# Rounding the queries and keys of one head one loop step later, in a fused causal attention and maxout FFN

## The chip, the cores and the metric

The kernel runs on 1 core of a Trainium2 chip. The metric is device time in microseconds (us), lower is better. Of the kernel before, three timed runs and one profiled execution are at hand.

## The reference

```python
# q, k, v: 8 batches x 8 heads x 576 x 64; s: 8 x 8 x 576; float32
scores = scale * np.matmul(q, k.transpose(0, 1, 3, 2))
cum = np.cumsum(np.maximum(s, 0.0), axis=-1)
bias = -(cum[:, :, :, None] - cum[:, :, None, :])
scores = np.where(causal, -1000000000.0, scores + np.minimum(bias, 0.0))
attn = np.exp(scores - np.max(scores, axis=-1, keepdims=True))
attn = attn / (np.sum(attn, axis=-1, keepdims=True) + 1e-09)
x = np.matmul(attn, v)                        # then 4608 tokens x 512
h = np.maximum(np.maximum(x @ w1, x @ w2), x @ w3)   # 512 -> 768
out = h @ w_out                                      # 768 -> 512
```

All 64 heads go through attention with a bias that decays with the distance, and the 4608 tokens then through a maxout layer of three matrices and an output matrix.

## The kernel before, in words

**Visits and steps.** Two heads are worked on together, a pair. A visit is one pair and a list of query blocks (128 queries each, the fifth 64): the first eight visits take blocks 0 and 1 of the first two batches, the next eight take their blocks 2, 3 and 4, and the last 24 visits ("stacked") take all five blocks of one pair. One query block of one visit is a step, 160 steps in all. The steps that matter here are 38 and 39 (blocks 3 and 4 of visit 15, the last that is not stacked), 40 to 44 (visit 16, the first stacked visit) and 45 to 49 (visit 17, the second).

**What a step is.** In turn t of the loop at L929 the kernel writes down, for all engines at once and in a fixed order: `probs(t)` (ACT rounds the normalized probabilities to a high float16 half `prh`, L512, and for block 4 a tail `tl`; DVE makes the low half `prl`, L515; SP's queue starts the DMA transposes of both into `ph` and `pl`, L518 to L528); `highest(t + 1)` (DVE, the row maximum, L457 or L462); the evictions that stand open (ACT L593 and L730, DVE L594 and L733, POOL L722 and L723); at most one group of FFN matmuls; `scores(t + 2)` (TensorE, L380, L391, L416); `expo(t + 1)` (ACT, L472 and L477); then a list of single jobs that a table `todo` holds for turn t; then more FFN groups, and after a visit's last block of a phase `values` (TensorE, L584, attention times values, from the transposed `ph`, `pl` and `tT`). Each engine runs its part strictly in this order, and so does SP's DMA queue. The scores live in PSUM in a ring of two buffers (`ps_s`), so `scores(t + 2)` writes the buffer that `probs(t)` has read last. `prh` and `prl` have two buffers each.

**What is prepared for a stacked visit, and when.** Each of its two heads j is loaded and rounded by itself. `load_head` (L121) starts two DMAs on SP's queue into a `raw` tile, of which there are two in a ring. `head_bias` (L128) fills bias rows of `l` with four POOL instructions (L141 to L147). `head_qhi` (L154, ACT) rounds the queries to `h`, `head_khi` (L158, ACT) the keys. `head_qlo` makes what the rounding of the queries left (L163, DVE) and copies a part of `h` into `l` (L167, POOL). `head_klo` makes the rest of the keys (L172, POOL); it is the last to read `raw`. The loop at L872 puts these jobs into `todo`: with o a turn number worked out from the visit's first step, at o `head_bias` and `head_qhi`, at o + 1 `head_khi` and `head_qlo`, at o + 2 `head_klo`, and the load one to three turns ahead of o. For the second stacked visit (n = 1, visit 17, whose first step is 45) head 0 has o = 37 and its load stands at 36.

**The FFN** runs as groups of 12 or 18 matmuls (L716 for the hidden layer, `pm`; L758 for the output, `po`) that a queue hands out by a count of estimated TensorE time; that count is worked out while the program is written, so it is the same in both kernels.

The loop that places the jobs is this, of the function printed below:

```python
for f, e in ((prep4, 1), (prep5, 0), (load, 7), (prep2, 4), (prep3, 3)):
    for v in range(len(visits)):
```

## Time and profile before

| what | value |
|---|---|
| median of three runs | 919.92 us (918.94 to 921.08) |
| the profiled execution | 914.14 us |
| its span, first to last instruction | 912.3 us |
| granted TensorE clock, mean | 0.963 |
| busy: TensorE, its weight loads, DVE, ACT, POOL | 90%, 71%, 66%, 62%, 38% |
| HBM over the span | 60.18 MB read, 9.44 MB written |

PE is TensorE, PEld its weight loads, DVE is VectorE, ACT ScalarE, POOL GpSimd, and SPq the queue of SyncE, from which nearly all DMAs start. A row of the timeline is: start, length, engine, line, operation, output<-input, shape, count, and in brackets the idle time of that engine just before it with what ended it. The chain of waits is followed back from the last instruction. Time outside the span is 914.14 - 912.3 = 1.84 us.

### The profile page before, as it was taken

The page shows a single profiled execution, that of the slowest core. Times are in us where ns is not written, and L with a number is a line of the kernel's source. Part 1 is how long each engine was busy: PE and PEld are TensorE (multiplying, and loading weights), DVE is VectorE, ACT ScalarE, POOL GpSimd, SP SyncE. Part 2 cuts the span into 40 slices and gives each one's busy share as a digit, 9 for nine tenths or more (in the row PEclk, how much of TensorE's full clock was granted, in tenths as well). Part 3 has the DMA queues.
Part 4 walks back from the last instruction along what each step waited for, and adds up shares of the span by engine and source line. Part 5 has one row for each costly group of instructions (what it writes and reads, how often), then busy time and mean ns, then how long its engine had stood idle before and what let it go on. Part 6 is the DMA issues. An engine that isn't in the chain of part 4 may idle for free.

```text
span 912.3 us, 19899 instructions
## 1 busy us (share of the span) xinstructions
PE 823.0 (90%) x7000; PEld 645.5 (71%) x7000; DVE 598.3 (66%) x1504; ACT 568.6 (62%) x1502; POOL 345.7 (38%) x553
## 2 busy tenths in 40 slices
PE   3557769998799989999999999999999999999998
PEld 2445657775467668867787778777787778777876
DVE  6898886666467766667676767676677657663111
ACT  4668577675566776666767677666677677764111
POOL 3111322223434444545353544445344536431211
PEclk9856989999999998999999999999999999999999
DMA  8963346666769768777878867777877677744000
GB/s 292 282 183 79 73 98 138 148 140 128 155 129 166 143 148 140 145 125 139 161 142 160 141 153 143 142 135 146 131 160 153 131 141 135 126 76 83 8 19 29
DMA packets 242036, 122.33 MB, mean 134 GB/s; under 512 B 217808, under 2 KB 226512, under 8 KB 241936
## 3 DMA queue, kind: packets, MB, share of 16 engines
q1 hardware_dynamic: 237904, 108.74, 60.8%
q10 hardware_dynamic: 4032, 12.32, 4.1%
q8 instruction: 55, 0.90, 0.5%
q14 instruction: 45, 0.37, 0.2%
HBM read 60.18 MB, written 9.44 MB: 76 GB/s over the span
## 4 chain that ended last, share of the span: by engine, by line
PE 69%; DMA 5%; DVE 4%; ACT 3%; issue 2%; POOL 2%; SPq 1%; ACTq 0%; DVEq 0%; POOLq 0%
PE pm L716 38%; PE po L758 13%; PE av L584 7%; PE s L380 6%; DMA ph<-prh 2%; PE s L391 2%; DMA pl<-prl 2%; DVE prl L515 2%; ACT prh L512 2%; PE s L416 1%; DVE m L733 1%; SPq L524 1%; POOL hh L722 1%; ACT s L472 1%; POOL hl L723 1%
## 5 line engine op out<-in xcount | busy, mean ns | idle before, releaser
L716 PE MATMUL pm<-x,w 128*128 128x256 f16 (+1 forms) x3456 | 455.9, 289 | 4.3 <-DVE m L733 2.2
L716 PEld LDWEIGHTS <-w 128*128 128x128 f16 x3456 | 330.9, 99 | 95.1 <-issue 8.9
L722 POOL CAST hh<-m 128x256 f16<-128x256 f32 (+1 forms) x96 | 55.4, 578 | 368.8 <-DVE m L733 310.3
L512 ACT ACTIVATE prh<-s,ri 128x512 f16<-128x512 f32 (+3 forms) x288 | 142.0, 539 | 80.8 <-DVE ri L496 71.6
L515 DVE SCALAR_TENSOR_TENSOR prl<-s,ri,prh 128x512 f16<-128x512 f32 (+3 forms) x288 | 152.9, 568 | 58.2 <-ACT prh L512 36.5
L733 DVE SCALAR_TENSOR_TENSOR m<-pm,m 128x256 f32<-128x256 f32 (+1 forms) x192 | 87.2, 454 | 125.1 <-PE pm L716 105.1
L472 ACT ACTIVATE s<-s,nm 128x512 f32<-128x512 f32 (+4 forms) x288 | 151.2, 525 | 12.3 <-DVE nm L457 5.6
L758 PE MATMUL po<-hh,w 128*128 128x256 f16 (+1 forms) x768 | 150.3, 288 | 0.0
L758 PEld LDWEIGHTS <-w 128*128 128x128 f16 x1152 | 110.4, 98 | 33.2 <-issue 5.0
L457 DVE CUSTOM_DVE_ANT_0 s<-s,later 128x128 f32<-128x128 f32 (+1 forms) x192 | 94.7, 493 | 33.4 <-PE s L380 30.0
L758 PE MATMUL po<-hl,w 128*128 128x320 f16 (+1 forms) x384 | 110.3, 287 | 1.5 <-POOL hl L723 1.4
L730 ACT ACTIVATE m<-pm 128x256 f32<-128x256 f32 (+1 forms) x96 | 39.1, 407 | 92.5 <-PE pm L716 88.2
L723 POOL TENSOR_TENSOR hl<-m,hh 128x256 f16<-128x256 f32 (+1 forms) x96 | 75.8, 790 | 7.8
L172 POOL TENSOR_TENSOR l<-raw,h 64x576 fp32r<-64x576 f32 x48 | 67.2, 1401 | 14.2 <-ACT h L158 12.8
L766 ACT ACTIVATE o<-po,os 128x256 f32<-128x256 f32 (+1 forms) x64 | 31.9, 499 | 62.2 <-PE po L758 53.2
L584 PE MATMUL av<-pl,vh 128*64 128x320 f16 (+3 forms) x384 | 59.6, 281 | 8.1 <-DMA pl<-prl 8.0
L462 DVE TENSOR_REDUCE nm<-s 128x1 f32<-128x576 f32 (+3 forms) x64 | 49.9, 780 | 22.1 <-PE s L396 12.3
L584 PEld LDWEIGHTS <-vh 128*64 128x64 f16 x832 | 47.8, 112 | 22.4 <-issue 11.1
L380 PE MATMUL s<-h 128*128 128x128 f32 (+1 forms) x192 | 54.2, 364 | 8.6 <-DVE prl L515 6.2
L584 PE MATMUL av<-ph,vh 128*64 128x320 f16 (+3 forms) x384 | 59.2, 288 | 1.1 <-DMA ph<-prh 0.8
L141 POOL CAST l<-kb 64x576 fp32r<-64x576 f32 x48 | 32.2, 672 | 73.2 <-PE s L391 71.9
L472 ACT ACTIVATION_READ_ACCUMULATOR s<-s,nm 128x1 f32 x288 | 57.3, 199 | 0.0
(140 smaller groups left out, 1090.3 us busy)
## 6 DMA issues: line engine op xcount, KB each, us to landing
raw<-in_qk_dram SPq DMA_DIRECT2D x96, 304.0 KB, 4.7
r<-in_w_dram ACTq DMA_DIRECT2D x20, 512.0 KB, 4.8
rv<-in_qkv_dram SPq DMA_DIRECT2D x32, 320.0 KB, 3.4
out_dram<-o SPq DMA_DIRECT2D x32, 160.0 KB, 2.1
out_dram<-o SPq DMA_DIRECT2D x32, 128.0 KB, 2.0
raw<-in_qkv_dram SPq DMA_DIRECT2D x8, 480.0 KB, 4.1
ph<-prh SPq DMA_TRANSPOSE x192, 3.4
pl<-prl SPq DMA_TRANSPOSE x192, 2.9
```

Of the source, the lines that this page charges most:

```text
L172: nc.gpsimd.tensor_tensor(out=l[far, QP:V0], in0=raw[far, QP:V0], in1=h[far, QP:V0].bitcast(F32), op=ALU.subtract)
L380: nc.tensor.matmul(ps[:, j, :nk], lhsT=w[:, qs], rhs=w[:, QP:QP + nk], start=(x == "h"), stop=(x == "l"), skip_group_check=True,)
L457: nc.vector.tensor_tensor_reduce(out=sc[:, j], in0=sc[:, j], in1=future[0][:, Q4 - nk:Q4], scale=-1.0, scalar=3.0e38, op0=ALU.add, op1=ALU ...
L472: nc.scalar.activation(out=sc, in_=sc, func=AF.Exp, bias=nm[:, j:j + 1], scale=-1.0 if below(t) else 1.0, accum_out=sm[:, j:j + 1],)
L512: nc.scalar.activation(out=hi, in_=src, func=AF.Copy, scale=sc)
L515: nc.vector.scalar_tensor_tensor(out=lo, in0=src, scalar=sc, in1=hi, op0=ALU.mult, op1=ALU.subtract)
L584: nc.tensor.matmul(av[j * D:(j + 1) * D, c0:nq], lhsT=lt, rhs=rt, start=(n < 2), stop=(n >= len(todo) - 2), skip_group_check=True,)
L716: nc.tensor.matmul(pm[:, :nq], lhsT=w[:, wt, kt, :], rhs=xt, start=(n == 0), stop=(n == 3 * NKT - 1))
L722: nc.gpsimd.tensor_copy(out=st["hh"][:, ft, :nq], in_=m1[:, :nq])
L723: nc.gpsimd.tensor_tensor(out=st["hl"][:, ft, :nq], in0=m1[:, :nq], in1=st["hh"][:, ft, :nq], op=ALU.subtract)
L733: nc.vector.scalar_tensor_tensor(out=m1[:, :nq], in0=pm[:, :nq], scalar=HSC, in1=m1[:, :nq], op0=ALU.mult, op1=ALU.max)
L758: nc.tensor.matmul(pm[:, :nq], lhsT=W[18 + ft][:, wt, dt, :], rhs=st[ht][:, ft, :nq], start=(n == 0), stop=(n == 3 * NFT - 1),)
```

## The change

Two lines are new and one is altered, all in the placing of the jobs:

```diff
                     o = first[v] - (8, 5)[j]
                     if n == 0:
                         o += 2 - j
+                    elif n == 1 and j == 0:
+                        o += 1
                     if f is load:
-                        at(o - (1 if n == 1 and j == 0 else 3 if n == 0 and j == 0 else 2), load_head, v, j)
+                        at(o - (3 if n == 0 and j == 0 else 2), load_head, v, j)
                     elif f is prep2:
                         at(o, head_bias, v, j)
                         at(o, head_qhi, v, j)
                         at(o + 1, head_khi, v, j)
                     else:
                         at(o + 1, head_qlo, v, j)
                         at(o + (1 if n == 0 else 2), head_klo, v, j)
```

For head 0 of visit 17 o becomes 38. The load stays in turn 36 (38 - 2 for 37 - 1). `head_bias` and `head_qhi` go from turn 37 to 38, `head_khi` and `head_qlo` from 38 to 39, `head_klo` from 39 to 40. SP's queue and TensorE keep their order; ACT, DVE and POOL do not. No instruction is added or removed.

On ACT, from the end of turn 37 on, before (`h_0` is the head that is moved, `h_1` head 1 of visit 16; the two `prh` are those of steps 38 and 39):

```order
L158 ACTIVATE h_1_3175<-raw_1_3004 128x576
L154 ACTIVATE h_0_3246<-raw_0_3172 128x640
L512 ACTIVATE prh_3287<-s_3149,ri_3285 128x4x128 x2
L593 ACTIVATE x_1_2829<-av_1_3256 128x320
L472 ACTIVATE s_3223,sm_3317<-s_3223,nm_3224 128x576
L477 ACTIVATE se_3319<-sm_3317 128x1
L730 ACTIVATE m_1_4_3321<-pm_1_4_0_3298 128x320
L158 ACTIVATE h_0_3246<-raw_0_3172 128x576
L512 ACTIVATE prh_3344<-s_3223,ri_3342 128x512
L512 ACTIVATE tl_3346<-s_3223,ri_3342 128x64
```

And now, in the same place:

```order
L158 ACTIVATE h_1_3175<-raw_1_3004 128x576
L512 ACTIVATE prh_3280<-s_3149,ri_3278 128x4x128 x2
L593 ACTIVATE x_1_2829<-av_1_3249 128x320
L472 ACTIVATE s_3223,sm_3310<-s_3223,nm_3224 128x576
L477 ACTIVATE se_3312<-sm_3310 128x1
L730 ACTIVATE m_1_4_3314<-pm_1_4_0_3291 128x320
L154 ACTIVATE h_0_3319<-raw_0_3172 128x640
L512 ACTIVATE prh_3341<-s_3223,ri_3339 128x512
L512 ACTIVATE tl_3343<-s_3223,ri_3339 128x64
```

The rounding of the queries, L154, has gone from ahead of the probabilities of step 38 to ahead of those of step 39, and L158 of the same head has left this stretch (it stands ahead of the probabilities of step 40). L163 on DVE has gone the same way.

On POOL, before, from turn 37 to the bias rows of the next head (`l_0` is the moved head, `l_1_3176` head 1 of visit 16, `l_1_3452` head 1 of visit 17):

```order
L141 CAST l_0_3247<-kb_175 64x576
L142 CAST l_0_3247<-qr_178 64x512
L146 MEMSET l_0_3247 64x64
L147 CAST l_0_3247<-qr_178 64x64
L167 CAST l_1_3176<-h_1_3175 64x640
L172 TENSOR_TENSOR l_1_3176<-raw_1_3004,h_1_3175 64x576
L167 CAST l_0_3247<-h_0_3246 64x640
L722 CAST hh_1_2901<-m_1_4_3321 128x320
L723 TENSOR_TENSOR hl_1_2902<-m_1_4_3321,hh_1_2901 128x320
L172 TENSOR_TENSOR l_0_3247<-raw_0_3172,h_0_3246 64x576
L141 CAST l_1_3452<-kb_175 64x576
```

And now, up to the same head's L172:

```order
L167 CAST l_1_3176<-h_1_3175 64x640
L172 TENSOR_TENSOR l_1_3176<-raw_1_3004,h_1_3175 64x576
L141 CAST l_0_3320<-kb_175 64x576
L142 CAST l_0_3320<-qr_178 64x512
L146 MEMSET l_0_3320 64x64
L147 CAST l_0_3320<-qr_178 64x64
L722 CAST hh_1_2901<-m_1_4_3314 128x320
L723 TENSOR_TENSOR hl_1_2902<-m_1_4_3314,hh_1_2901 128x320
L167 CAST l_0_3320<-h_0_3319 64x640
L141 CAST l_1_3451<-kb_175 64x576
L142 CAST l_1_3451<-qr_178 64x512
```

The four bias instructions of the moved head stand behind L167 and L172 of visit 16 instead of ahead of them, its L167 behind an FFN pair instead of ahead of it, and its L172 (not shown) behind the four bias instructions of the next head instead of ahead of them. On SP's queue the load of visit 18's head 0, in turn 40, waits for that L172, since it takes the same `raw` buffer.

Of the kernel before, what the change touches and what calls it, by code (L numbers as in the profile page):

```python
# [21 lines left out]
def kernel(  # L22
# [95 lines left out]
    def stacked(v):  # L118
        return len(visits[v][2]) == 5
# [99 lines left out]
    for j in range(2):  # L219
        nc.gpsimd.memset(ones[64 * j + 32:64 * j + 64, 0:1], 1.0)  # L220
        nc.gpsimd.memset(ones[64 * j:64 * j + 32, 1:2], 1.0)
        for T in range(2):
            a = 32 * j + 16 * T
            for c in range(2):
                o = 32 + 64 * j + 16 * c
# [594 lines left out]
    def at(t, f, *a):  # L820
        todo.setdefault(t, []).append((f, a))
# [50 lines left out]
    for f, e in ((prep4, 1), (prep5, 0), (load, 7), (prep2, 4), (prep3, 3)):  # L872
        for v in range(len(visits)):
            t = first[v] - e
            if v % NP == 0 and f in (prep4, prep5):
                t = first[v] + 1 + (f is prep5) if v else -1
            if f is prep5 and v >= NP and v + NP < len(visits):
                at(t, f, v)
                at(t, load_v, v + NP)
                continue  # L880
            if f is load and NP <= v < 2 * NP:
                t = first[v] - 6
            if 2 * NP * NB - 2 <= v < 2 * NP * NB and f in (load, prep2, prep3):
                t = first[v] - (8 if f is load else 4 if f is prep3 and v % 2 == 0 else 5)
            if stacked(v) and f in (load, prep2, prep3):
                n = v - 2 * NP * NB
                for j in range(2):
                    o = first[v] - (8, 5)[j]
                    if n == 0:
                        o += 2 - j  # L890
                    if f is load:
                        at(o - (1 if n == 1 and j == 0 else 3 if n == 0 and j == 0 else 2), load_head, v, j)
                    elif f is prep2:
                        at(o, head_bias, v, j)
                        at(o, head_qhi, v, j)
                        at(o + 1, head_khi, v, j)
                    else:
                        at(o + 1, head_qlo, v, j)
                        at(o + (1 if n == 0 else 2), head_klo, v, j)
                continue  # L900
            at(t, f, v, *([nc.scalar.dma_start] if f is load and v < NP + 2 else []))
# [121 lines left out]
```

## The prediction

> **What bounds the kernel now.** I read the page first, then the chain of waits, then the waits, the granted clock and the timeline around the place where the moved instructions stand.
>
> ```profile
> PE 823.0 (90%) x7000; PEld 645.5 (71%) x7000; DVE 598.3 (66%) x1504; ACT 568.6 (62%) x1502; POOL 345.7 (38%) x553
> ...
> PE 69%; DMA 5%; DVE 4%; ACT 3%; issue 2%; POOL 2%; SPq 1%; ACTq 0%; DVEq 0%; POOLq 0%
> ```
>
> TensorE sets the pace over most of the span: it is busy 90% of it and holds 69% of the chain. Time saved elsewhere counts only where TensorE stands idle for it. The moved instructions run between 239 and 260 us. The chain of waits there:
>
> ```profile
> 242.66 4.57 DMA raw<-in_qk_dram
> ...
> 247.98 1.26 ACT prh L512 x2
> ...
> 249.26 1.42 DVE prl L515 x2
> 250.68 0.14 issue
> 250.82 1.09 PE s L380 x4
> 251.91 4.63 PE pm L716 x24
> 256.54 0.47 PE s L380 x4
> 257.01 3.29 PE pm L716 x24
> ...
> 275.95 0.50 PE s L380 x4
> ```
>
> The chain leaves TensorE for a load of `raw`, which lands at 242.66 + 4.57 = 247.23, goes over ACT's `prh` and DVE's `prl` of step 38, and comes back to TensorE at 250.82 with `scores(40)`. The waits between 239 and 251 us say the same:
>
> ```profile
> ACT h L154 <- DMA raw<-in_qk_dram: 7.6, 1, 7.6
> DVE prl L515 <- ACT prh L512: 6.9, 1, 6.9
> ...
> PE s L380 <- DVE prl L515: 5.3, 1, 5.3
> ```
>
> The `raw` that lands is that of visit 17, which TensorE does not need until step 45. ACT takes its instructions in order, so L154, waiting for this load, holds up `prh` of step 38 behind it, whose inputs have long been there. That is the wait which the change takes from this place. The timeline of TensorE, then of ACT:
>
> ```profile
> 242.19 0.30 PE L584 MATMUL av<-pl,vh 128*64 128x320 f16 x1 [1.45 <-DMA pl<-prl]
> ...
> 243.68 1.80 PE L716 MATMUL pm<-x,w 128*128 128x320 f16 x12
> ...
> 262.99 0.33 PE L584 MATMUL av<-ph,vh 128*64 128x320 f16 x2
> 263.15 0.30 PE L584 MATMUL av<-pl,vh 128*64 128x320 f16 x2
> ```
>
> ```profile
> 239.06 0.67 ACT L158 ACTIVATE h<-raw 128x576 fp32r<-128x576 f32 x1
> 247.34 0.74 ACT L154 ACTIVATE h<-raw 128x640 fp32r<-128x640 f32 x1 [7.60 <-DMA raw<-in_qk_dram]
> ...
> 251.90 0.69 ACT L512 ACTIVATE prh<-s,ri 128x512 f16<-128x512 f32 x1 [0.49 <-DVE ri L496]
> ```
>
> TensorE ends its group at 243.68 + 1.80 = 245.48 and starts `scores(40)` at 250.82: 5.34 us idle. Between 239.73 and 247.34 ACT does nothing. The clock that TensorE is granted in the stages around it (third column from the right):
>
> ```profile
> 246.00:250.80 4.80, 0.00 (x0) 0.01 (x1) 1.54 (x3) 3.43 (x9) 0.72 (x1) 0.68 0.77 162
> 250.80:252.00 1.20, 1.18 (x6) 1.08 (x7) 1.12 (x4) 0.71 (x3) 0.00 (x0) 0.50 0.95 174
> 252.00:257.00 5.00, 5.00 (x30) 3.37 (x29) 2.52 (x9) 1.84 (x7) 0.00 (x0) 0.75 1.02 200
> ```
>
> After the idle time TensorE runs at half its clock and on the whole at 0.75 for the next 5 us, so the stall costs more than its own length.
>
> **The change part by part.** All times of the new run are worked out on the profiled execution, by moving these rows.
>
> *The idle time.* With L154 gone from ahead of it, `prh` of step 38 waits for the reciprocal `ri` on DVE, and then `scores(40)` for `prl` of step 38 and for `l` of visit 16's head 1, which POOL's L172 finishes. Rows of DVE, then of POOL:
>
> ```profile
> 241.58 0.17 DVE L496 RECIPROCAL ri<-se 128x2 f32<-128x2 f32 x1
> ...
> 250.98 0.81 DVE L163 SCALAR_TENSOR_TENSOR h<-raw,h 64x640 fp32r<-64x640 f32 x1
> ...
> 252.82 0.75 DVE L515 SCALAR_TENSOR_TENSOR prl<-s,ri,prh 128x512 f16<-128x512 f32 x1
> 253.49 0.27 DVE L515 SCALAR_TENSOR_TENSOR tl<-s,ri,tl 128x64 f16<-128x64 f32 x1
> ...
> 256.57 0.49 DVE L733 SCALAR_TENSOR_TENSOR m<-pm,m 128x320 f32<-128x320 f32 x1 [1.06 <-PE pm L716]
> 256.98 0.81 DVE L293 TENSOR_REDUCE am<-rv 128x1 f32<-128x640 f32 x1
> ...
> 258.63 0.61 DVE L515 SCALAR_TENSOR_TENSOR prl<-s,ri,prh 128x128 f16<-128x128 f32 x2
> ```
>
> ```profile
> 242.15 0.66 POOL L141 CAST l<-kb 64x576 fp32r<-64x576 f32 x1
> ...
> 243.57 0.71 POOL L167 CAST l<-h 64x640 fp32r<-64x640 f32 x1
> 244.25 1.39 POOL L172 TENSOR_TENSOR l<-raw,h 64x576 fp32r<-64x576 f32 x1
> ```
>
> `ri` ends at 241.75; 1.26 us of `prh`, 1.42 of `prl` and 0.14 of issue give 244.57. L172 ends at 245.64 now; the four bias instructions ahead of it (242.15 to 243.57, 1.42 us) go behind it, so it ends at 244.22. Both are ahead of 245.48, so the whole 5.34 us go.
>
> *The clock.* Without the idle time the four score matmuls take the 0.50 us of their like at 275.95 instead of 1.09, and the 24 matmuls 3.29 us (the next 24, at 257.01) instead of 4.63: 0.59 + 1.34 = 1.93 us. The Trainium skill, "TensorE: Matmul & The Clock Gate", Part 1: The HAM clock gate, says that the array's clock is halved after an idle window of about 3.4 us and restored after a busy one of the same length. The 0.50 after 5.34 us agrees; by the page the stall would cost 3.4 x 0.5 = 1.7 us of clock, an estimate, and the total below would be 4.8 in place of 5.0.
>
> So TensorE is ahead by up to 5.34 + 1.93 = 7.27 us. Three things are late next.
>
> *L154 in its new place, ahead of `prh` of step 39.* It still waits for the load, which nothing moves (SP's order is the same and no row ahead of 242 us changes): it starts at 247.34, `prh` of step 39 at 247.98. From the start of `prh` to the end of the tail on DVE it is 253.76 - 251.90 = 1.86 us, with the issue 249.98. TensorE is ready for `scores(41)` at 245.48 + 0.50 + 3.29 = 249.27. New idle time: 0.71 us.
>
> *L163 and L158 one step later.* L163 now stands ahead of the reciprocal of step 40. From the FFN eviction at 256.57 to the end of `prl` of step 40 at 259.24 it is 2.67 us, with L163's 0.81 in it 3.48. The two evictions follow the tail (249.84) at once, the second after 0.41 (256.57 to 256.98): `prl` ends at 249.84 + 0.41 + 3.48 = 253.73, with issue 253.87. TensorE gets to `scores(42)` at 249.98 + 0.47 + 3.29 = 253.74. New idle time: 0.13 us. L158 (0.67 us on ACT) stands ahead of `prh` of step 40, which waits for that reciprocal in any case: nothing.
>
> *SP's queue.* The attention values of visit 15 need the transposes of step 39, and SP can't give back all of the stall:
>
> ```profile
> 237.65 2.48 SPq L524 DMA_TRANSPOSE pl<-prl  x2
> ...
> 246.36 0.57 SPq L111 DMA_DIRECT2D rv<-in_qkv_dram  x1
> 249.25 1.25 SPq L518 DMA_TRANSPOSE ph<-prh  x1
> ...
> 255.90 2.48 SPq L524 DMA_TRANSPOSE pl<-prl  x2
> ...
> 262.33 1.97 SPq L125 DMA_DIRECT2D raw<-in_qk_dram  x2
> ```
>
> SP was issuing other transfers until 246.93 and waited only from there to 249.25, so its row moves up by 2.32 us, and the last `pl` of step 39 is issued by 258.38 - 2.32 = 256.06. In step 36 such a transpose was issued by 240.13 and let TensorE go on at 242.19, 2.06 us later; here that is 258.12. TensorE gets to its first `pl` matmul at 263.15 - (7.27 - 0.71 - 0.13) = 256.72. New idle time: 1.40 us, short of the stall that it replaces.
>
> *The bias rows and L172 of the moved head.* POOL has them done long before visit 17's first step; that SP's load for visit 18 (262.33) now waits for this L172 is weighed below.
>
> The sum: 5.34 + 1.93 - 0.71 - 0.13 - 1.40 = 5.03 us. From there on every engine is ahead by this much and all orders are as before, so it should reach the end. The profiled execution, 914.14, would become 909.1. The median of the runs shown is 5.78 above it; I leave that difference as it is: 919.92 - 5.0 = 914.9.
>
> Bounds of what the trace does not show: the new waits could be nothing, 7.27 us in all; or the sixteen DMA engines, not SP's issue, set when `pl` lands. They were idle for 23% of 4.8 us ahead of 250.8, 1.10 us, and full behind it (0.95, 1.02), so the landing would move up by 1.10 instead of 2.32 and the sum be 3.8. I take SP's figure, since in step 36 the landing followed the issue by 2.06 us, with the issue rows back to back.
>
> **The rivals.** *All of it stays:* 7.27 us, 912.6, if `pl` lands 1.4 us earlier than in step 36 and `raw` 0.7 earlier. Against it: SP's rows have no gap to close after 249.25.
>
> *DMA-bound:* 3.8 us, 916.1, as above. For it speaks the share of 1.02, against it that TensorE at 262.99 did not wait for `ph` or `pl`, so that there was room.
>
> *Taken back later:* the gain is given back at a transfer that TensorE waits for further on (5% of the chain is DMA): 919.9. Against it: those transfers are issued out of the same rows that move up.
>
> *Slower, by the load behind L172.* SP's load for visit 18 can't start before the moved head's L172 on POOL, and the transposes of step 41 stand behind it on SP. POOL does the FFN pair and L167, then four bias instructions (1.42 us) and L172 (1.39): it starts the pair at about 250.7 when DVE has evicted (249.84 + 0.41 + 0.49), and even at 2 us for pair and L167 (an estimate from its 0.71 us for L167) ends by 255.6. SP reaches the load at 262.33 - 2.32 = 260.0. It decides only if POOL is over 4.4 us later than that, and the kernel is slower than before by 1.84 us only at 4.4 + 5.0 + 1.84 = 11.3 us: then 921.8 or more. No row near it speaks for that.
>
> That the change does nothing is excluded: the order on ACT is another one, and the wait stood there.
>
> **How the numbers follow.** The forecast, 914.9, has 0.58; DMA-bound 0.16; all of it stays 0.09; taken back 0.12; slower 0.05. A measurement of this kernel can tell 0.2%, 1.84 us, from no change. The range goes from all of it (912.6) to DMA-bound (916.1); the runs shown lie up to 1.2 us from their median, and half of a later loss (2.5 us of 5.0) ends at 917.4, so I give 912.4 to 917.8; 0.17 is left out. Faster: 0.58 + 0.16 + 0.09 = 0.83, and of the loss taken back in part 0.02 more, 0.85; same 0.10; slower 0.05.
>
> **What would show it.** In the new profile: TensorE's idle time ahead of `scores(40)` gone, with the clock near 1 from 245 to 257 us; ACT's wait for `raw` still there, ahead of `prh` of step 39, about 1.5 us long; a wait of TensorE for `pl` ahead of the values of visit 15 near 257 us. The reading is wrong if `scores(40)` still waits for `prl`, if the load of `raw` lands later than 247.3, or if the lead of TensorE at 270 us is well under 4 and the span shows it again at a wait further on.

## The result, and the profile after

| | kernel before | changed kernel |
|---|---|---|
| median of the runs, first comparison | 919.43 us (917.26 to 921.08, 4 runs) | 912.76 us (912.39 to 914.09, 4 runs) |
| ratio | | 0.9937, 95% interval 0.9909 to 0.9964 |
| second comparison | 917.64 us (15 runs) | 912.65 us (8 runs) |
| ratio | | 0.9954, 0.9934 to 0.9975 |
| the profiled execution | 914.14 us | 913.03 us |

The changed kernel is faster, by 5.8 us by the first ratio and 4.2 by the second, and neither interval reaches 1. The two profiled executions differ by 1.11 us alone, which has to be explained too. The page after:

```profile
PE 824.4 (90%) x7000; PEld 646.9 (71%) x7000; DVE 599.1 (66%) x1504; ACT 570.2 (63%) x1502; POOL 346.3 (38%) x553
...
PE 67%; DMA 6%; DVE 4%; ACT 4%; issue 2%; POOL 2%; SPq 1%; POOLq 0%; DVEq 0%; ACTq 0%
```

As a whole it reads as before. The chain of waits around the place does not:

```profile
242.78 2.25 PE av L584 x23
245.03 2.65 PE pm L716 x12
247.69 0.39 PE s L380 x4
248.08 3.29 PE pm L716 x24
...
256.13 3.97 DMA pl<-prl
260.11 0.04 issue
260.15 1.57 PE av L584 x23
```

The load of `raw` has left the chain: `scores(40)` (247.69) follows its FFN group at once, and the 24 matmuls behind it take 3.29 us where they took 4.63. What holds TensorE next is `pl` of step 39. The timeline of TensorE's score and value matmuls, with its idle times in brackets:

```profile
247.42 0.44 PE L380 MATMUL s<-h 128*128 128x128 f32 x2
...
251.09 0.51 PE L380 MATMUL s<-h 128*128 128x256 f32 x2
...
255.55 0.59 PE L380 MATMUL s<-h 128*128 128x384 f32 x2 [0.44 <-ACT s L472]
...
260.15 0.30 PE L584 MATMUL av<-pl,vh 128*64 128x320 f16 x1 [1.57 <-DMA pl<-prl]
```

5.34 us of idle time are gone, 0.44 and 1.57 are new (`scores(42)` and the values of visit 15). ACT in the same stretch:

```profile
239.45 0.67 ACT L158 ACTIVATE h<-raw 128x576 fp32r<-128x576 f32 x1
242.01 1.27 ACT L512 ACTIVATE prh<-s,ri 128x512 f16<-128x512 f32 x2 [1.90 <-DVE ri L496]
...
248.12 0.73 ACT L154 ACTIVATE h<-raw 128x640 fp32r<-128x640 f32 x1
248.75 0.68 ACT L512 ACTIVATE prh<-s,ri 128x512 f16<-128x512 f32 x1
```

`prh` of step 38 runs at 242.01 instead of 247.98, and L154, in its new place, finds its load landed.

To see how far a gain lasts, each execution is cut at the row `se` on ACT, of which every step has one. These are steps 38, 43 and 64, of before and then of after:

```profile
238.96 0.20 ACT L477 ACTIVATE se<-sm 128x2 f32<-128x2 f32 x1
...
271.63 0.20 ACT L477 ACTIVATE se<-sm 128x2 f32<-128x2 f32 x1
...
370.46 0.20 ACT L477 ACTIVATE se<-sm 128x1 f32<-128x1 f32 x1
```

```profile
239.33 0.21 ACT L477 ACTIVATE se<-sm 128x2 f32<-128x2 f32 x1
...
268.62 0.20 ACT L477 ACTIVATE se<-sm 128x2 f32<-128x2 f32 x1
...
369.71 0.20 ACT L477 ACTIVATE se<-sm 128x1 f32<-128x1 f32 x1
```

The differences of these starts, in us, for every profiled execution of the study (the last column goes to the end of the span):

| execution | start to 38 | 38 to 43 | 38 to 64 | 64 to end |
|---|---|---|---|---|
| before | 238.96 | 32.67 | 131.50 | 541.86 |
| before, again | 239.09 | 34.39 | 134.62 | 541.36 |
| bias rows alone | 243.62 | 32.61 | 134.16 | 541.53 |
| changed | 239.33 | 29.29 | 130.38 | 541.51 |
| changed, again | 236.94 | 29.58 | 130.23 | 541.45 |
| other data | 241.09 | 28.95 | 128.25 | 541.63 |
| L154 alone | 238.24 | 28.69 | 130.16 | 541.41 |
| load earlier | 240.75 | 28.87 | 129.06 | 541.48 |
| both heads later | 239.88 | 27.46 | 129.23 | 542.60 |
| L163 and L167 back | 239.82 | 28.24 | 129.13 | 542.15 |
| both of these | 240.09 | 28.01 | 130.84 | 543.34 |
| load later | 242.50 | 37.40 | 136.00 | 541.86 |
| L172 later | 238.45 | 29.03 | 140.12 | 542.09 |

Up to step 38 the executions scatter over 6.7 us, though all but the one with the earlier load are alike there. After step 64 most lie within half a microsecond. The change shows in the middle columns: 33.2 us from 38 to 43 in the first three rows, which have the stall, 29.4 in the two of the changed kernel, 27.5 to 29.6 in the eight rows from the changed kernel to both of these, which do not. From 38 to 64 the means are 133.4 and 129.7, 3.8 us apart. Between 43 and 64 the four with the stall (the load one turn later among them) take 99.8 us in the mean, 98.6 to 101.6, and the eight without it 101.0, 99.3 to 102.8: a part of the gain seems to go again there, within the scatter. So a single pair of profiled executions can hide the gain: the one of before that was shown is the shortest of its three from 38 to 64, and the changed one lost time again near 284 us, as told below. The two last rows of the table are the ones made slower, and are told with their experiments.

### The profile page after: what moved, and what is told of

It reads as the page before. It is cut to its first block, busy times and chain, and to the rows that moved or that the text cites. A ratio compares the mean times of both kernels' runs of the same rounds, so it can differ in the third digit from the quotient of the medians.

```text
span 911.2 us, 19898 instructions
## 1 busy us (share of the span) xinstructions
PE 824.4 (90%) x7000; PEld 646.9 (71%) x7000; DVE 599.1 (66%) x1504; ACT 570.2 (63%) x1502; POOL 346.3 (38%) x553
## 4 chain that ended last, share of the span: by engine, by line
PE 67%; DMA 6%; DVE 4%; ACT 4%; issue 2%; POOL 2%; SPq 1%; POOLq 0%; DVEq 0%; ACTq 0%
PE pm L716 37%; PE po L758 13%; PE av L584 7%; PE s L380 6%; DMA pl<-prl 3%; PE s L391 2%; DMA ph<-prh 2%; DVE prl L515 1%; ACT prh L512 1%; PE s L416 1%; ACT s L472 1%; DMA tT<-tl 1%; DVE m L733 1%; SPq L524 1%; POOL hh L722 1%
## 5 line engine op out<-in xcount | busy, mean ns | idle before, releaser
L723 POOL TENSOR_TENSOR hl<-m,hh 128x256 f16<-128x256 f32 (+1 forms) x96 | 76.1, 792 | 7.8
L172 POOL TENSOR_TENSOR l<-raw,h 64x576 fp32r<-64x576 f32 x48 | 67.2, 1400 | 12.3 <-ACT h L158 11.0
L584 PE MATMUL av<-pl,vh 128*64 128x320 f16 (+3 forms) x384 | 61.7, 286 | 8.6 <-DMA pl<-prl 8.3
L593 ACT ACTIVATE x<-av 128x256 f16<-128x256 f32 (+1 forms) x64 | 26.3, 411 | 52.7 <-PE av L584 51.6
L584 PE MATMUL av<-ph,vl 128*64 128x320 f16 (+3 forms) x384 | 58.2, 287 | 0.0
```

The lines of the kernel that those rows point to most:

```text
L172: nc.gpsimd.tensor_tensor(out=l[far, QP:V0], in0=raw[far, QP:V0], in1=h[far, QP:V0].bitcast(F32), op=ALU.subtract)
L584: nc.tensor.matmul(av[j * D:(j + 1) * D, c0:nq], lhsT=lt, rhs=rt, start=(n < 2), stop=(n >= len(todo) - 2), skip_group_check=True,)
L723: nc.gpsimd.tensor_tensor(out=st["hl"][:, ft, :nq], in0=m1[:, :nq], in1=st["hh"][:, ft, :nq], op=ALU.subtract)
```

## The experiments

The theory was: TensorE stood idle ahead of `scores(40)` because ACT, in order, waited in L154 for a load that nobody needed yet. The rivals were that the order on POOL or DVE brings the gain, and, on the slower side, that SP's load for visit 18 gets held by the later L172. Each ratio below is to runs of the kernel before in the same comparison; the experiments fall into three such comparisons, and the changed kernel was in one of them, so ratios of different comparisons are set side by side with their intervals.

**The kernel before, again.** No edit.

> The kernel before, unchanged, to see how its profiled executions differ: the one shown took 914.14 us, its timed runs 917.3 to 921.1, while the changed kernel's profiled execution took 913.03 and its runs 912.4 to 914.1. The stall theory (the gain is TensorE's idle time ahead of scores(40), made by ACT's wait for raw) expects a span between 915 and 919 us with that idle time above 5.3 us, since the load lands later in it; the rival that the runs gain somewhere else expects about 5.3 us there again and the missing microseconds in another stretch. The ratio to the kernel before is 1.000 within 0.002 by both.

Ratio 1.0009 (0.9995 to 1.0022), span 915.1 us. The stall is there, at 5.69 us:

```profile
251.64 0.66 PE L380 MATMUL s<-h 128*128 128x128 f32 x2 [5.69 <-DVE prl L515]
```

Neither expectation holds alone: from 38 to 43 it is 1.7 us longer than in the first execution, and 1.4 us more go between 43 and 64. The time of one execution is no measure of a change of this size here; the ratios are.

**The wait taken away, and nothing moved.** In `head_qhi`, for visit 17's head 0 alone:

```diff
         raw, h = R[v]["raw", j], R[v]["h", j]
+        if (v, j) == (2 * NP * NB + 1, 0):
+            raw = R[v - 1]["raw", 1]
```

> The kernel before in which the queries of visit 17's head 0 are rounded from the raw tile of visit 16's head 1, which landed long ago: no instruction moves, only the wait of L154 for its load goes. Its output for this one head is that of other queries. Stall theory: as fast as the changed kernel, ratio 0.992 to 0.995. Rival (the order on POOL or DVE brings the gain): 0.999 to 1.001.

Ratio 0.9958 (0.9940 to 0.9975), as the changed kernel within the intervals, at the upper edge of what was expected. With every instruction in its old place the gain comes from ACT's wait alone. DVE's L163 still reads the tile of its own load and waits 1.09 us for it, and TensorE is idle 0.74 us ahead of `scores(41)`.

**The bias rows alone.** Their four instructions go into a function of their own, called one turn later for this head:

```diff
+                        if n == 1 and j == 0:
+                            at(o + 1, head_fill, v, j)
```

> The kernel before with the four bias instructions of visit 17's head 0 alone one turn later, on POOL; ACT and DVE as before. Stall theory: 0.999 to 1.001, since scores(40) waits for prl until 250.8 and l of visit 16 is done by 245.6 already. Rival (POOL's order brings the gain): 0.992 to 0.996.

Ratio 1.0006 (0.9990 to 1.0021), and the stall stays (lines of this kernel are five further down):

```profile
254.69 0.66 PE L385 MATMUL s<-h 128*128 128x128 f32 x2 [4.55 <-DVE prl L520]
```

The order on POOL brings nothing by itself.

**L154 alone.**

```diff
-                        at(o, head_qhi, v, j)
+                        at(o + (1 if n == 1 and j == 0 else 0), head_qhi, v, j)
```

> The kernel before with L154 of visit 17's head 0 alone one turn later; the bias rows, L158, L163, L167 and L172 as before. Stall theory: nearly all of the gain, 0.992 to 0.996: L163 now waits on DVE for L154 (248.0 us) ahead of the reciprocal of step 39, which costs 0 to 1 us. Rival (POOL's or DVE's order brings the gain): 0.998 to 1.002.

Ratio 0.9950 (0.9935 to 0.9965). This one instruction is the change; the rest of the move (bias rows, L158, L163, L167, L172) adds nothing that these runs can tell.

**The load one turn earlier**, instead of the rounding one turn later:

```diff
-                        at(o - (1 if n == 1 and j == 0 else 3 if n == 0 and j == 0 else 2), load_head, v, j)
+                        at(o - (3 if n == 0 and j == 0 else 2), load_head, v, j)
```

> The kernel before with the load of visit 17's head 0 one turn earlier (35) in place of the rounding one turn later: the same distance of two turns between load and rounding, made from the other side. Stall theory: the load is issued behind the transposes of step 35, near 235 us, and lands near 240, so L154 waits 0 to 1 us; the transposes of step 36 come 1.2 us later, which the values of visit 14 wait for; ratio 0.993 to 0.997. Rival (it matters what stands where on ACT, DVE and POOL, not when the load lands): 0.999 to 1.001.

Ratio 0.9958 (0.9942 to 0.9974). What counts is the distance between the load and the instruction that waits for it; from which side it is made is no difference that these runs can tell.

**The load one turn later**, on the kernel before:

```diff
-                        at(o - (1 if n == 1 and j == 0 else 3 if n == 0 and j == 0 else 2), load_head, v, j)
+                        at(o - (0 if n == 1 and j == 0 else 3 if n == 0 and j == 0 else 2), load_head, v, j)
```

> The kernel before with the load of visit 17's head 0 one turn later (37) and the rounding where it was (37): the wait of L154 made longer. SP would issue the load behind the transposes of step 37 and a load of values, about 4.3 us later than before. Stall theory: L154's wait and TensorE's idle time ahead of scores(40) grow by about 4.3 us each and the kernel by 3 to 4.5 us, ratio 1.003 to 1.005. Rival (the wait is made good further on, since transposes are waited for there in any case): 0.999 to 1.002.

Ratio 1.0067 (1.0050 to 1.0084), 6.1 us slower. ACT's wait and TensorE's:

```profile
255.89 0.74 ACT L154 ACTIVATE h<-raw 128x640 fp32r<-128x640 f32 x1 [12.61 <-DMA raw<-in_qk_dram]
```

```profile
259.37 0.66 PE L380 MATMUL s<-h 128*128 128x128 f32 x2 [10.53 <-DVE prl L515]
```

The waits grew by 5.0 and 5.2 us, more than the 4.3 expected, and the kernel by more than the 3 to 4.5. With idle times of 0, 5.34 and 10.53 us it stands at -4.2 (the second ratio), 0 and +6.1 us: 0.8 us for each microsecond of idle time on the first step and 1.2 on the second.

**The changed kernel, again.** No edit.

> The changed kernel, unchanged, for a closer ratio. The sum of the prediction, 5.0 us of 919, is a ratio of 0.9945; the first timing gave 0.9937 within 0.9909 to 0.9964. Stall theory: 0.993 to 0.996, and in the profile no idle time of TensorE ahead of scores(40), but 1 to 2 us of it for pl at the values of visit 15. Rival (the first timing was helped by chance in the early steps): 0.997 to 1.000.

Ratio 0.9954 (0.9934 to 0.9975), in the expected range. The idle times of TensorE are those of the first execution: none ahead of `scores(40)`, 0.44 us ahead of `scores(42)`, and

```profile
258.05 0.30 PE L584 MATMUL av<-pl,vh 128*64 128x320 f16 x1 [1.92 <-DMA pl<-prl]
```

**L172 two turns later still**, on the changed kernel, so that SP's load has to wait:

```diff
-                        at(o + (1 if n == 0 else 2), head_klo, v, j)
+                        at(o + (1 if n == 0 else 4 if n == 1 and j == 0 else 2), head_klo, v, j)
```

> The changed kernel with L172 of visit 17's head 0 two turns later still (42 in place of 40), so that SP's load for visit 18, in turn 40, must wait for it: the prediction's rival on the slower side, made on purpose. L172 would end near 272 us, and SP reaches the load at 262: about 10 us of SP standing still, with the transposes of step 41 behind it. If that gate works as the prediction has it: 3 to 9 us slower than the changed kernel, ratio to the kernel before 0.998 to 1.005, and TensorE idle at the values of visit 16's first phase for ph or pl. Rival (the load's wait hides, the transposes of step 41 are not needed so soon): 0.993 to 0.996, as the changed kernel.

Ratio 1.0063 (1.0042 to 1.0084) against 0.9954 of the changed kernel in the same comparison: 10.0 us slower than that, where 3 to 9 were expected. SP's queue, and TensorE at the values of visit 16:

```profile
259.69 1.20 SPq L518 DMA_TRANSPOSE pl<-prl  x1
271.50 1.10 SPq L125 DMA_DIRECT2D raw<-in_qk_dram  x2
272.70 1.22 SPq L518 DMA_TRANSPOSE ph<-prh  x1
```

```profile
277.22 0.42 PE L584 MATMUL av<-ph,vh 128*64 128x256 f16 x2 [8.58 <-DMA ph<-prh]
```

SP stands from 260.89 to 271.50, and the transposes of step 41 behind the load come too late. The gate is real and dear; one turn, as the change has it, stays clear of it (L172 ends at 257.34 in the changed kernel, and SP comes to the load at 262.14).

Up to turn 40 this run has the instructions of the changed kernel, and its clock is granted in full from 137.32 to 270.44 us. So it shows the new waits of the prediction undisturbed, on ACT and then on TensorE ahead of `scores(41)`, `scores(42)` and at the values of visit 15:

```profile
247.54 0.74 ACT L154 ACTIVATE h<-raw 128x640 fp32r<-128x640 f32 x1 [1.45 <-DMA raw<-in_qk_dram]
```

```profile
250.21 0.48 PE L380 MATMUL s<-h 128*128 128x256 f32 x2 [0.84 <-ACT se L477]
...
254.72 0.59 PE L380 MATMUL s<-h 128*128 128x384 f32 x2 [0.52 <-ACT s L472]
...
259.01 0.30 PE L584 MATMUL av<-pl,vh 128*64 128x320 f16 x1 [1.26 <-DMA pl<-prl]
```

**Head 1 of visit 17 one turn later too**, on the changed kernel:

```diff
-                    elif n == 1 and j == 0:
+                    elif n == 1:
...
-                        at(o + (1 if n == 0 else 2), head_klo, v, j)
+                        at(o + (1 if n == 0 or n == 1 and j == 1 else 2), head_klo, v, j)
```

> The changed kernel with head 1 of visit 17 one turn later as well (its load in turn 39, rounding in 41, L172 in 42): SP then issues the transposes of step 39 ahead of that load, so pl of step 39 should land 1.2 us earlier. If SP's issue sets the wait at the values of visit 15, as the prediction has it, that wait falls by about 1.2 us and the kernel is 1 us faster than the changed one, ratio 0.992 to 0.995. Rival (the sixteen DMA engines or the later turns set it, or head 1 comes too late for scores(45)): no faster than the changed kernel, 0.994 to 0.998.

With the load of head 1 behind the transposes of step 39, TensorE's wait for `pl` is gone and 0.35 us for the tail is left:

```profile
260.12 0.22 PE L584 MATMUL av<-tT,vh 128*64 128x64 f16 x2 [0.35 <-DMA tT<-tl]
```

So that load, ahead of the transposes on SP's queue, did set that wait, and the stretch from 38 to 43 is 2 us shorter. Whether by the 1.2 us of its issue or by its transfer this run can't tell: the mean busy share of the sixteen DMA engines between 250 and 254 us fell with it, from 1.10 in the changed kernel to 0.86. The time is not: 0.9948 (0.9930 to 0.9967), beside 0.9954 for the changed kernel. The expectation was right on the size of the wait, and whether a microsecond of it reaches the end these runs can't tell.

**L163 and L167 back in turn 38**, on the changed kernel:

```diff
-                        at(o + 1, head_qlo, v, j)
+                        at(o + (0 if n == 1 and j == 0 else 1), head_qlo, v, j)
```

> The changed kernel with L163 and L167 of visit 17's head 0 back in turn 38. In the changed kernel L163 (DVE) takes 1.42 us in place of 0.81 while L167 (POOL) takes 1.19 in place of 0.71 beside it, and TensorE is idle 0.44 us ahead of scores(42), where the prediction had 0.13. If the two hold each other up, moving both away from there brings L163 back under 1.0 us and the idle time under 0.2; in return DVE waits for L154 ahead of the reciprocal of step 39, 0 to 0.5 us at scores(41). Ratio 0.993 to 0.997, the changed kernel within 0.5 us. Rival (L163 is long for another reason): it stays at 1.4 us.

Ratio 0.9960 (0.9945 to 0.9975). L163 is back at 0.82 us and no idle time is left ahead of `scores(42)`; ahead of `scores(41)` it is 1.95 us, more than the 0.5 expected, since DVE now waits 2.67 us for L154:

```profile
249.44 0.82 DVE L163 SCALAR_TENSOR_TENSOR h<-raw,h 64x640 fp32r<-64x640 f32 x1 [2.67 <-ACT h L154]
```

```profile
252.38 0.48 PE L380 MATMUL s<-h 128*128 128x256 f32 x2 [1.95 <-ACT se L477]
```

**Both of these together.** The last two edits on one kernel.

> Both changes together: head 1 of visit 17 one turn later as well, which took the wait for pl at the values of visit 15 from 1.6 to 0.35 us, and L163 and L167 of head 0 in turn 38. If the two gains add: 38 to 43 in 27 us (33.2 in three executions of the kernel before, 29.4 in two of the changed one), ratio 0.992 to 0.995. Rival (what is gained there is given back by turn 64, as in the run with head 1 later): 0.994 to 0.997.

Ratio 0.9957 (0.9943 to 0.9972), 28.0 us from 38 to 43, 130.84 from 38 to 64. In these single executions the gains don't add. No version was found that is faster than the changed kernel beyond the intervals.

## Why the prediction was right, point by point

**The bound** was right: a load that was not yet needed held ACT, and through `prh` and `prl` TensorE. Taking that wait alone away, or L154 alone out of the way, or the load forward, gives 0.9950 to 0.9958, and the order on POOL alone 1.0006.

**The idle time, 5.34 us**, went as worked out: `scores(40)` has no wait in any of the nine executions in which L154, its load or its wait was moved out of the way.

**The clock, 1.93 us**, is the term that was mis-sized. Its place was right: `scores(40)` to `scores(41)` take 5.17 to 6.47 us in the four executions with the stall and 3.67 in both of the changed kernel. The stretch behind `scores(40)` runs at the full clock now, but in both executions of the changed kernel the clock was halved somewhat earlier, where it had not been before. The windows of the changed kernel (the third column from the right is the granted clock; the number ahead of the first bracket is TensorE's busy time):

```profile
240.05:243.46 3.41, 1.51 (x18) 1.04 (x18) 2.67 (x5) 1.33 (x3) 3.25 (x4) 1.00 0.19 34
243.46:246.88 3.42, 3.42 (x27) 2.48 (x23) 1.91 (x4) 1.36 (x4) 2.42 (x5) 0.50 0.85 196
246.88:250.29 3.41, 3.41 (x28) 2.61 (x27) 1.34 (x5) 2.47 (x8) 0.00 (x0) 1.00 0.98 187
281.01:284.42 3.41, 1.61 (x11) 1.03 (x11) 2.50 (x7) 1.58 (x3) 2.33 (x3) 1.00 0.43 38
284.42:287.84 3.42, 3.42 (x28) 2.87 (x28) 0.94 (x3) 0.54 (x2) 1.63 (x5) 0.50 0.32 84
```

TensorE waited 1.90 us for `pl` at the values of visit 14, and the 3.42 us after that window ran at half the clock: 1.7 us lost. That wait was there before the change as well (1.45 us), without this consequence. So of the 1.93 us some 0.2 were gained in this execution. In the other one of the changed kernel the halved window starts at 240.44, after one with 1.75 us busy, and in the one with L154 alone at 242.89; the six others without the stall have none near there, and gain the term. None of the four with the stall has one ahead of the stall; whether the change makes it more frequent stays open.

A second halved window, at 284.42, is where the first execution of the changed kernel lost most of its lead: 3.01 us at the score matmuls that start at 284.02 in before, 0.09 at those that start at 289.11, about half of it by longer waits at the values of visit 16 (0.99 us where before had 0.26, and 0.81 for `pl` where it had none) and half by the clock.

**L154 in its new place, 0.71 us ahead of `scores(41)`:** 0 in the changed kernel, since the halved clock brought ACT there late (248.12) and the load had landed; where the clock was full, L154 waited 1.45 us and TensorE 0.84 (L172 two turns later), or 1.41 and 0.93 (both heads later), near what was worked out.

**L163, 0.13 us ahead of `scores(42)`:** 0.44 in both executions of the changed kernel, 0.52 with L172 later. The length of L163 was taken from the old place and is not that in the new one:

```profile
252.53 1.42 DVE L163 SCALAR_TENSOR_TENSOR h<-raw,h 64x640 fp32r<-64x640 f32 x1
```

```profile
252.48 0.79 POOL L723 TENSOR_TENSOR hl<-m,hh 128x320 f16<-128x320 f32 x1
253.34 1.19 POOL L167 CAST l<-h 64x640 fp32r<-64x640 f32 x1
```

It starts 0.05 us after POOL's L723 and takes 1.42 us instead of 0.81; L167 starts inside it and takes 1.19 instead of 0.71. With L163 ahead of its neighbour on POOL, in the run with L163 and L167 back, it takes 0.82, and L167, which starts 0.10 us after it, 1.31. The Trainium skill, "SBUF — State Buffer", section "SBUF: two separate sides", says that a DVE operation with two inputs in SBUF and a GpSimd operation that reads SBUF share a port pair as an exclusive lock, for whichever starts first; 1.42 against 0.82 for L163, and 1.19 and 1.31 against 0.71 for L167, agree with that. It was left out of the sum.

**SP's queue, 1.40 us at the values of visit 15:** 1.57 and 1.92, and 1.26 with L172 later. That it comes so near is in part luck, since both sides of the difference came late. Counted from the row `se` of step 38, TensorE was to reach this matmul after 17.76 us and `pl` to release it after 19.16; in the two executions of the changed kernel TensorE came after 19.25 and 19.19 us, and `pl` after 20.82 and 21.11. SP was late already ahead of the transposes of step 38 (its row L111 ends 8.84 and 9.35 us after that mark, 7.97 in before), and `pl` released TensorE 2.77 and 2.52 us after its issue, where 2.06 was taken over from step 36. That the order on SP's queue sets the wait was shown by moving one load behind the transposes; that it is the issue, and not the transfers, is argued, not shown.

**The bias rows and the load behind L172:** no cost, as worked out, with the gate shown by the run that closes it.

**The sum**, 5.03 us, stands against 5.8 us (3.3 to 8.4, the interval times 919.43) and 4.2 (2.3 to 6.1) in the two timings, 3.8 from 38 to 64 by the means of the profiled executions. In the single profiled execution it is 3.38 from 38 to 43 (32.67 - 29.29), short by the clock. There TensorE's lead at the scores near 270 us is 3.01 us, under the 4 that the prediction named, and the span keeps 1.1 of it: by that execution alone its sign of being wrong would nearly have been met. The ratios, and the other executions, say otherwise.

**The rivals.** DMA-bound (3.8 us) and all of it (7.3) are not told apart from 5.0 by the times alone, but by the trace all of it does not hold, since the wait for `pl` is there. DMA-bound is left open. Its wait, 1.40 + 1.22 = 2.62 us, is longer than the 1.26 to 1.92 of these executions, but its landing, 20.4 us after the mark, is nearer to what `pl` did than the forecast's 19.16. Taken back later happened in part: at the values of visit 16 TensorE waits 0.70 to 0.86 us for `pl` in seven of the eight executions from the changed kernel to both of these, and in one of the four with the stall (0.80, before, again); in the first execution of the changed kernel the clock took more. The prediction had no term for this: it let the whole lead of 5.03 us reach the end.

## What to carry to other kernels

On an engine that works in order, look for the instruction that waits for data nobody needs yet, and count what is queued behind it; the fix is the distance to its load, from either side. Where one execution scatters by more than the gain, cut the executions at marks that all kernels share and compare the stretch that was touched. A duration from the old place need not hold in the new one when the neighbour on another engine changes.

## What the runs showed of the hardware that was not expected

The granted clock is halved in whole windows of 3.41 us, and the idle window of the rule that the prediction draws on is not needed for it: windows in which TensorE was busy 1.51 and 1.61 us of 3.41 were each followed by one at 0.50. A window of the kernel before with 2.11 us busy was followed by a full one:

```profile
240.89:244.30 3.41, 2.11 (x30) 1.92 (x30) 1.47 (x3) 0.00 (x0) 3.35 (x7) 1.00 0.30 78
244.30:247.72 3.42, 1.18 (x9) 0.62 (x7) 0.00 (x0) 0.38 (x1) 1.34 (x1) 1.00 1.11 215
247.72:251.13 3.41, 0.31 (x2) 0.34 (x2) 1.87 (x4) 3.38 (x9) 0.72 (x1) 0.50 0.59 153
251.13:254.55 3.42, 3.42 (x15) 2.27 (x15) 2.39 (x8) 2.23 (x8) 0.00 (x0) 0.50 0.90 185
254.55:257.96 3.41, 3.41 (x28) 2.55 (x26) 1.88 (x5) 0.06 (x1) 0.68 (x2) 1.00 0.94 168
```

These rows alone would put a border between 1.61 and 2.11 us of 3.41, but the thirteen traces have none so sharp. Of their 3066 windows at the full clock all 58 with less than 1.42 us busy were followed by a halved one, and none of the 2836 with 2.48 us or more. Of those between, 24 were and 148 were not; in the run with the load one turn earlier the window at 96.66, with 1.42 us busy, was followed by a full one, and the next, at 100.07, with 2.47 us busy, by a halved one. So busy time as the profile has it does not settle it alone. A halved window that is busy throughout costs 1.7 us, half of 3.41, and of two waits at the values of visit 14 the one of 1.90 us, in the changed kernel, was followed by one, and the one of 2.00 us, in the run with both of these, was not. That where a wait falls against the windows decides this is argued from the traces and was not tried by itself.
